# Attention and feed-forward in one kernel: score and state products of four pairs joined into one piece of TensorE work each

## The chip, the cores and the metric

The kernel runs on one core of one Trainium2 chip. The time is the device time of one execution in microseconds; the median of three executions is given, and a profiled execution is used to see where the time goes. Engines are named as in the profile: PE is TensorE (matmul), PEld its weight load, DVE VectorE, ACT ScalarE, POOL GpSimd, SP the engine that issues most DMAs.

## The reference

Linear attention with a decay per head, followed by a feed-forward block that is computed per token. The inputs are q, k and v of 4 batches, 8 heads, 768 tokens and 64 channels, in float32.

```python
for b in range(nb):                       # blocks of 64 tokens
    intra = einsum('bhic,bhjc->bhij', qb, kb) * Dmask      # scores, masked and decayed
    intra = einsum('bhij,bhjd->bhid', intra, vb)
    inter = einsum('bhid,bhde->bhie', qb * lam_pow, kv_state)
    out[:, :, sl] = intra + inter
    kv_state = lam_block * kv_state + einsum('bhsd,bhse->bhde', kb * rev_pow, vb)
x = out.transpose(0, 2, 1, 3).reshape(4, 768, 512)
xn = (x - mean(x)) / sqrt(var(x) + 1e-6) * g_ln
out = x + relu(xn @ w_ch1) @ w_ch2        # 512 -> 2048 -> 512
```

## The kernel before

The work is cut into 12 units of 256 tokens of one batch, called pairs here because each is a pair of 128-token chunks (`ab` 0 and 1); they are counted from 0, so the third to sixth are pairs 2 to 5. Pair u belongs to batch u mod 4, and the state of a batch is handed from pair u to pair u + 4. The steps of a pair are:

- loads of k, q and v by DMA from SP, in float32 (`load_in`, L76 and L80);
- scaling and conversion to bf16: `in_k_one` (L229, L213), `in_q_one` (L234) and `in_v` (L240), on POOL, ACT or DVE, into the tiles `kq` and `vb`;
- transposing k and q: by PE in pairs 0 to 2 (`transpose_pe`), by DMA from SP in the others (`transpose_dma`, L255, one DMA for k and one for q), into `kqT`;
- state products `kv` (L305): 32 matmuls in 64x64 tiles of the array, into two PSUM buffers `pk`. The argument names the buffers: "mm" is a rotating set of four that the feed-forward products use too, "po" are the two buffers of the attention's output;
- score products `scores` (L271), in two halves of 16 matmuls, also in 64x64 tiles, into two buffers of the tag "sc", or with `early=True` into two of the "mm" set;
- `mask` (L281) on DVE, from PSUM to `mA`; two per half;
- `new_state`: DVE adds the new products to the old state (`state_sum`, L315, or L311 where there is no old state), and POOL applies the decay (L311);
- `av` (L417) and `inter` (L430): the attention's output in `po`, again in 64x64 tiles;
- `norm`: ACT copies `po` to `x` with a row sum (L456), DVE forms `xc` (L458);
- `to_xT`: transposing `xc` for the feed-forward block; by PE (L491) into a "po" buffer in pairs 2, 3 and 4 with a copy by ACT (L492), by DMA (L484) from pair 5 on;
- `rstd_of`: the row's standard deviation on ACT (L501, L502), its reciprocal on DVE (L506).

Pairs 6 to 11 use other forms of the same steps (`kv64` L370, `scores64` L351, `av64` L404).

The feed-forward block of a pair is a list of units: `m1` (L528, 8 matmuls over the whole array, and a relu on ACT, L531) and, for pairs 0 to 3, `m2` (L665, 4 matmuls with 512 columns; after the fourth unit DVE adds the residual in `finish`, L689). From pair 4 on the second product is done with seven half products instead of eight (`m2w`, L563), for which sums over the second weight are formed once on DVE (`w_sums`, L787 to L791). All of these units stand in one plan, and `units(n)` takes the next n of them.

The order of the instructions on each engine is the order in which the program calls these functions; it is written out by hand at the end of the kernel. Each engine works through its instructions in that order. So where a call stands decides what lies between two attention steps on PE, and also what stands behind what on DVE, ACT, POOL and in SP's queue of DMAs.

The calls around pair 3 show the manner (lines 1083 to 1099, the casts of pair 5 left out):

```python
    w_sums(1, 0)
    units(3)
    s1(3)        # kv, scores of the first half, new_state, masks
    store(0)
    units(2)
    s2(3)        # scores of the second half, masks
    units(1)
    ...
    units(1)
    s3(3)        # av, first part of inter
    units(1)
    s4(3)        # second part of inter, norm
```

Of the kernel before, what the change touches and what calls it, by code (L numbers as in the profile page):

```python
# [8 lines left out]
BF16 = mybir.dt.bfloat16  # L9
# [8 lines left out]
def kernel(  # L18
# [11 lines left out]
    nc = tc.nc  # L30
# [7 lines left out]
    NP = H // 2  # L38
# [13 lines left out]
    wk = ctx.enter_context(tc.tile_pool(name="wk", bufs=2))  # L52
# [9 lines left out]
    def mm_tile(shape, dtype, name):  # L62
        return ps.tile(shape, dtype, tag="mm", bufs=4, name=name)
# [126 lines left out]
    st = {}  # L190
# [60 lines left out]
    def transpose_dma(u, a):  # L251
        s = st[u]
        if "kqT" not in s:
            s["kqT"] = wk.tile([128, 2, NP, 2, 128], BF16, tag="kqT", bufs=3, name="kqT")
        nc.sync.dma_start_transpose(s["kqT"][:, a].rearrange("p b j t -> p (b j) t"),  # L255
                                    s["kq"][:, a].rearrange("p b j e d -> p (b j e d)"))

    def scores(u, hf, early=False):

        s = st[u]  # L260
        kT, qT = s["kqT"][:, 0], s["kqT"][:, 1]
        if early:
            sc = [mm_tile([128, 2, 2, 128], F32, f"sce{e}") for e in range(2)]
        else:
            sc = [ps.tile([128, 2, 2, 128], F32, tag="sc", bufs=2, name=f"sc{e}") for e in range(2)]
        mA = wk.tile([128, 2, 2, 2, 128], BF16, tag=f"mA{hf}", name=f"mA{hf}")
        for i in range(2):
            for jk in range(2):
                for ab in range(2):
                    for e in range(2):  # L270
                        nc.tensor.matmul(sc[e][half[ab], i, jk, :], lhsT=kT[half[e], 2 * hf + i, jk, half[ab]],  # L271
                                         rhs=qT[half[e], 2 * hf + i, :, half[ab]],
                                         start=(i == 0 and jk == 0), stop=(i == 1 and jk == 1), skip_group_check=True)
        s[f"mA{hf}"] = mA
        s[f"sc{hf}"] = sc

    def mask(u, hf, heads=(0, 1)):
        s = st[u]
        kp = keep.rearrange("p a b t -> p a (b t)")
        for e in heads:  # L280
            nc.vector.tensor_tensor(s[f"mA{hf}"][:, e], s[f"sc{hf}"][e],  # L281
                                    kp[:, None, :, :].to_broadcast([128, 2, 2, 128]), op=ALU.mult)
# [11 lines left out]
    def kv(u, tag="mm"):  # L294

        s = st[u]
        cc, b = divmod(u, B)
        n_ab = 2 if (cc + 1) * W < S else 1
        bufs = dict(mm=4, sc=2, po=1)[tag]
        pk = [ps.tile([128, 2, NP, D], F32, tag=f"po{ab}" if tag == "po" else tag, bufs=bufs, name=f"pk{ab}")[:, 0] for ab in range(n_ab)]  # L300
        for p in range(NP):
            for j in range(2):
                for e in range(2):
                    for ab in range(n_ab):
                        nc.tensor.matmul(pk[ab][half[e], p, :], lhsT=s["kq"][half[ab], 0, p, j, e],  # L305
                                         rhs=s["vb"][half[ab], 2 * p + e, j],
                                         start=(p == 0 and j == 0), stop=(p == NP - 1 and j == 1), skip_group_check=True)
        s["pk"] = pk

    def decay(eng, dst, src):  # L310
        eng.tensor_tensor(dst, src, lam_s[:, :, None].to_broadcast([128, NP, D]), op=ALU.mult)  # L311
# [6 lines left out]
    def new_state(u, ab, eng):  # L318

        s = st[u]  # L320
        b = u % B
        if ab == 1 and len(s["pk"]) == 1:
            return
        old = state.get(b)
        if ab == 0:
            s["S"] = [(old, old)]
        Sn = wk.tile([128, NP, D], BF16, tag="S", bufs=12, name="Sn")
        if old is None and eng is nc.scalar:
            for p in range(NP):
                nc.scalar.activation(Sn[:, p], s["pk"][ab][:, p], ACT.Identity, scale=lam_s[:, p:p + 1])  # L330
        elif old is None:
            decay(nc.vector, Sn, s["pk"][ab])
        else:
            tmp = s.pop("tmp", None) or state_sum(u, ab)
            decay(eng, Sn, tmp)
        state[b] = Sn
        if ab == 0:
            s["S"].append((Sn, Sn))
# [136 lines left out]
    def to_xT(u, ab):  # L475
        s = st[u]
        t = 2 * u + ab
        g = group_of[t]
        i = t - groups[g][0]
        if i == 0:  # L480
            xT_of[g] = gp.tile([128, KA, GT * 128], BF16, tag="xT", bufs=3, name="xT")
        dst = xT_of[g][:, :, i * 128:(i + 1) * 128]
        if u >= 2 and u not in X_PE:
            nc.sync.dma_start_transpose(dst, s["xc"][:, ab])  # L484
        else:
            if u < 2:
                xt = mm_tile([128, KA, 128], BF16, "xt")
            else:
                xt = ps.tile([128, KA, 128], BF16, tag=f"po{ab}", name="xt")
            for kk in range(KA):  # L490
                nc.tensor.transpose(xt[:, kk, :], s["xc"][:, ab, kk * 128:(kk + 1) * 128], ident)  # L491
            nc.scalar.copy(dst, xt)  # L492

    def rstd_of(u):
        s = st[u]
        std = wk.tile([128, 2], F32, tag="std", name="std")
        if "sum" in s:
            ss = xp.tile([128, 2], F32, tag="ss", name="ss")
            for ab in range(2):
                sq = wk.tile([128, DM], BF16, tag="sq", bufs=1, name="sq")  # L500
                nc.scalar.activation(sq, s["x"][:, ab], ACT.Square, bias=s["nmean"][:, ab:ab + 1], accum_out=ss[:, ab:ab + 1])  # L501
            nc.scalar.activation(std, ss, ACT.Sqrt, bias=eps_t, scale=XS * XS / DM)  # L502
        else:
            nc.scalar.activation(std, s["mv"][:, :, 1], ACT.Sqrt, bias=eps_t, scale=XS * XS)
        rstd = xp.tile([128, 2], F32, tag="rstd", name="rstd")
        nc.vector.reciprocal(rstd, std)  # L506
        x_keep[u] = (s["x"], rstd)
# [187 lines left out]
    def store(u):  # L695
        for j in range(2):
            nc.sync.dma_start(rows_of(u)[j], o_of[u][half[j]])
# [83 lines left out]
    def w_sums(c, n):  # L781
        v = w2[c].rearrange("p (k e) d -> p k e d", e=2)
        w = DM // 2
        b11, b12, b21, b22 = v[:, :, 0, 0:w], v[:, :, 0, w:], v[:, :, 1, 0:w], v[:, :, 1, w:]
        t1, t2, t3, t4 = (wt[c][:, :, i] for i in range(4))
        if n == 0:
            nc.vector.tensor_tensor(t1, b12, b11, op=ALU.subtract)  # L787
            nc.vector.tensor_tensor(t3, b12, b22, op=ALU.add)
        else:
            nc.vector.tensor_tensor(t2, b11, t3, op=ALU.subtract)  # L790
            nc.vector.tensor_tensor(t4, t2, b21, op=ALU.add)  # L791
# [19 lines left out]
    def s0(u):  # L811
        kv(u, "po")
        new_state(u, 0, nc.gpsimd)
        new_state(u, 1, nc.gpsimd)
# [5 lines left out]
    def s1(u):  # L820
        kv(u)
        scores(u, 0)
        new_state(u, 0, nc.gpsimd)
        mask(u, 0, (0,))
        new_state(u, 1, nc.gpsimd)
        mask(u, 0, (1,))

    def wind_up(u):
# [22 lines left out]
        for ab in range(2):  # L851
            x, xh = s["x"][:, ab], s["x"][:, ab].rearrange("p (a e d) -> p a e d", e=2, d=D)
            nc.scalar.copy(x, s["po"][ab].rearrange("p h d -> p (h d)"))
            if has[ab]:
# [7 lines left out]
            nc.vector.scalar_tensor_tensor(s["xc"][:, ab], in0=x, scalar=s["mv"][:, ab, 0:1], in1=g_row,  # L862
                                           op0=ALU.subtract, op1=ALU.mult)

    def s2(u):
        scores(u, 1)
        mask(u, 1)
# [11 lines left out]
    def s4(u):  # L879
        inter(u, 1)  # L880
        if st[u]["S"][0][1] is not None:
            norm(u, 0)
        norm(u, 1)
# [142 lines left out]
    def units(n):  # L1026
        for _ in range(n):
            f, *a = next(steps)
            f(*a)
# [9 lines left out]
    s1b(2)  # L1039
    units(2)  # L1040
    s2(2)
    nc.scalar.activation(sqrt_first, eps_t, ACT.Sqrt)
    rstd_of(0)
    rstd_of(1)
    units(2)
    s0(2)
    open_window(3)
    in_k_one(3, nc.gpsimd, 0)
    in_k_one(3, nc.gpsimd, 1)
# [32 lines left out]
    units(2)  # L1082
    w_sums(1, 0)
    units(3)
    s1(3)
    store(0)
    units(2)
    s2(3)
    units(1)
    open_window(5)  # L1090
    in_k_one(5, nc.gpsimd, 0)
    in_k_one(5, nc.gpsimd, 1)
# [4 lines left out]
    s3(3)  # L1097
    units(1)
    s4(3)
    rstd_of(3)  # L1100
    open_in(6, False)
    load_in(6, "k", nc.sync)
    units(1)
    load_in(6, "q", nc.sync)
    units(1)
    w_sums(1, 1)
    load_in(6, "v", nc.sync)
    units(1)
    transpose_dma(5, 0)
    units(1)  # L1110
    to_xT(3, 0)
    transpose_dma(5, 1)
    open_in(7, False)
    load_in(7, "k", nc.sync)
    units(1)
    s1(4)
    to_xT(3, 1)
    open_window(6)
    in_k_one(6, nc.scalar, 0)
    units(1)  # L1120
    in_k_one(6, nc.gpsimd, 1)
    units(2)
    open_window(7)
    s2(4)
    units(2)
    s3(4)
    units(1)
# [11 lines left out]
    units(1)  # L1139
    open_in(8, False)  # L1140
    to_xT(4, 0)
    units(1)
    to_xT(4, 1)
    s1(5)
    units(1)
    transpose_dma(6, 1)
    units(1)
    in_q_one(7, nc.gpsimd, 0)
    units(1)
    in_q_one(7, nc.gpsimd, 1)  # L1150
    s2(5)
    transpose_dma(6, 0)
    units(2)
    rstd_of(4)
# [124 lines left out]
    in_k_one(11, nc.scalar, 0)  # L1279
    units(1)  # L1280
    in_k_one(11, nc.scalar, 1)
    transpose_dma(11, 0)
    transpose_dma(11, 1)
    units(1)
    m2s[8].sums(0, 4)
    units(1)
# [71 lines left out]
```

## Time and profile before

| | |
|---|---|
| time, median of 3 | 210.82 us (210.16 to 210.96) |
| the profiled execution | 209.44 us, its span 207.7 us |
| mean granted TensorE clock | 0.995 |
| PE busy | 197.0 us, 95% of the span |
| DVE, ACT, POOL busy | 134.3, 121.5, 86.0 us |
| bytes moved | 36.39 MB, 175 GB/s on average |

The span is the time from the first to the last instruction in the profiled execution. The chain of work that ended last is followed back from the last instruction, at each step to what released it; a row of it gives a start, a duration and what it was. Rows of a timeline give start, duration, engine, line, operation, output and inputs, and in brackets how long the engine had stood idle and what ended that. Starts and durations are in us from the start of the span. The chain counts each instruction only from the moment at which it is the one that matters, so its pieces lie end to end; the timeline gives each instruction's whole duration, and those overlap on PE.

### The profile page before, as it was taken

How to read it: one execution, taken by the hardware profiler on the slowest of the kernel's cores; microseconds unless marked ns; L12 is line 12 of the kernel's file. 1: busy time of each engine (PE TensorE's matmuls, PEld its weight loads, DVE VectorE, ACT ScalarE, POOL GpSimd, SP SyncE). 2: the span in 40 equal slices, each digit the busy share in tenths (PEclk: the TensorE clock that was granted, in tenths of full speed). 3: DMA queues.
4: the chain of work that ended last, by engine and by line, in shares of the span. 5: the costliest groups of instructions: out<-in, count | busy, mean ns of one | idle time of the engine just before them, and what ended most of it. 6: DMA issues, size and time to landing. Idle time of an engine off the chain costs nothing.

```text
span 207.7 us, 7234 instructions
## 1 busy us (share of the span) xinstructions
PE 197.0 (95%) x3099; PEld 156.3 (75%) x3099; DVE 134.3 (65%) x274; ACT 121.5 (58%) x279; POOL 86.0 (41%) x119
## 2 busy tenths in 40 slices
PE   2989999999999999999999999999999999999991
PEld 0468788545774587488888888888888888888880
DVE  2588350625864949767898775786877947855262
ACT  3776479535357457257565775585586565752620
POOL 5558049237784540635264441772182202001020
PEclk9999999999999999999999999999999999999997
DMA  4999999999898999996899999898957020268403
GB/s 106 299 257 218 193 269 186 187 289 260 202 261 248 228 137 229 188 290 109 180 199 145 190 196 173 211 190 145 227 98 171 4 51 3 28 157 273 105 13 90
DMA packets 91042, 36.39 MB, mean 175 GB/s; under 512 B 65153, under 2 KB 88193, under 8 KB 91010
## 3 DMA queue, kind: packets, MB, share of 16 engines
q1 hardware_dynamic: 86400, 31.53, 74.1%
q0 software_dynamic: 4224, 4.19, 12.7%
q8 instruction: 24, 0.39, 0.8%
q10 hardware_dynamic: 386, 0.20, 0.4%
q14 instruction: 8, 0.07, 0.1%
HBM read 27.27 MB, written 6.29 MB: 162 GB/s over the span
## 4 chain that ended last, share of the span: by engine, by line
PE 84%; DMA 5%; DVE 4%; ACT 3%; issue 1%; POOL 0%; POOLq 0%; DVEq 0%
PE pm L528 38%; PE pm L665 14%; PE pwd L563 6%; PE pwa L563 6%; PE pwc L563 6%; DMA w<-in_moe_w_ch_dram 3%; PE pwb L563 3%; DMA lam_b<-in_lam_dram 2%; PE po L417 2%; PE po L430 1%; PE tp L248 1%; PE sc L271 1%; DVE x L576 1%; PE po L404 1%; PE sc L351 1%
## 5 line engine op out<-in xcount | busy, mean ns | idle before, releaser
L528 PE MATMUL pm<-xT,w 128*128 128x256 bf16 x736 | 85.1, 273 | 0.6 <-DMA w<-in_moe_w_ch_dram 0.4
L528 PEld LDWEIGHTS <-w 128*128 128x128 bf16 x736 | 70.3, 98 | 10.5 <-DMA w<-in_moe_w_ch_dram 0.6
L531 ACT ACTIVATE hT<-pm 128x512 f16<-128x512 f32 x92 | 54.0, 599 | 32.6 <-PE pm L528 32.5
L665 PE MATMUL pm<-w,hT 128*128 128x512 f16 x128 | 30.2, 380 | 0.0
L588 POOL TENSOR_TENSOR x<-ev_u,x 128x256 f32<-128x256 f32 x8 | 5.8, 725 | 51.8 <-ACT ev_u L587 40.5
L563 PEld LDWEIGHTS <-hs 128*128 128x128 f16 x256 | 24.9, 98 | 2.9
L546 DVE TENSOR_TENSOR hs<-hT 128x1024 f16<-128x1024 f16 x16 | 14.1, 881 | 16.6 <-ACT hT L531 16.6
L311 POOL TENSOR_TENSOR Sn<-Stmp,lam_s 128x256 bf16<-128x256 f32 x16 | 9.8, 616 | 31.4 <-DVE Stmp L389 18.4
L665 PEld LDWEIGHTS <-hT 128*128 128x128 f16 x128 | 11.7, 98 | 12.1
L563 PEld LDWEIGHTS <-hT 128*128 128x128 f16 x192 | 18.8, 98 | 2.2
L281 DVE TENSOR_TENSOR mA<-sc,keep 128x512 bf16<-128x512 f32 x20 | 13.1, 684 | 10.4 <-PE sc L271 10.3
L458 DVE SCALAR_TENSOR_TENSOR xc<-po,nmean,g_row 128x512 bf16<-128x512 f32 x18 | 13.0, 746 | 5.0 <-ACT nmean L457 4.9
L456 ACT ACTIVATE x<-po 128x512 f32<-128x512 f32 x18 | 10.6, 590 | 8.0 <-PE po L430 4.5
L240 POOL TENSOR_TENSOR vb<-vin,lam_v 128x1024 bf16<-128x1024 f32 (+1 forms) x7 | 11.6, 1659 | 5.0 <-DMA vin<-in_v_dram 4.8
L240 POOL TENSOR_TENSOR vb<-vin,lam_p 128x1024 bf16<-128x1024 f32 x6 | 11.7, 1954 | 3.4 <-DMA vin<-in_v_dram 3.4
L501 ACT ACTIVATE sq<-x,nmean 128x512 bf16<-128x512 f32 x18 | 12.9, 718 | 0.3
L576 DVE SCALAR_TENSOR_TENSOR x<-pwd,rstd,x 128x256 f32<-128x256 f32 x16 | 7.7, 482 | 3.6 <-POOL x L596 3.6
L234 POOL TENSOR_TENSOR kq<-qin,lam_p 128x512 bf16<-128x512 f32 x9 | 9.3, 1042 | 1.1 <-DMA qin<-in_q_dram 1.1
L234 POOL TENSOR_TENSOR kq<-qin,lam_q 128x512 bf16<-128x512 f32 x8 | 8.6, 1089 | 2.8 <-DMA qin<-in_q_dram 2.8
L576 DVE SCALAR_TENSOR_TENSOR x<-pwa,rstd,x 128x512 f32<-128x512 f32 (+1 forms) x16 | 9.1, 613 | 0.8
L563 PE MATMUL pwa<-w,hT 128*128 128x256 f16 x64 | 9.6, 272 | 0.0
L563 PE MATMUL pwb<-w,hT 128*128 128x256 f16 x64 | 9.2, 272 | 0.0
(131 smaller groups left out, 297.5 us busy)
## 6 DMA issues: line engine op xcount, KB each, us to landing
out_dram<-x SPq DMA_DIRECT2D x22, 256.0 KB, 3.9
w<-in_moe_w_ch_dram POOLq DMA_DIRECT2D x8, 512.0 KB, 7.8
kin<-in_k_dram SPq DMA_DIRECT2D x14, 256.0 KB, 5.3
qin<-in_q_dram SPq DMA_DIRECT2D x14, 256.0 KB, 4.8
vin<-in_v_dram SPq DMA_DIRECT2D x14, 256.0 KB, 5.1
kin<-in_k_dram SPq DMA_DIRECT2D x5, 512.0 KB, 6.2
qin<-in_q_dram SPq DMA_DIRECT2D x5, 512.0 KB, 7.0
vin<-in_v_dram SPq DMA_DIRECT2D x5, 512.0 KB, 7.8
```

The lines of the kernel that those rows point to most:

```text
L234: eng.tensor_tensor(part(1, st[u]["kq"], ALL)[:, :, :, j], src[:, :, :, j], lq[:, :, :, None].to_broadcast([128, NP, 2, D]), op=ALU.mult)
L240: eng.tensor_tensor(st[u]["vb"][:, hs], qkv_in[u]["v"][:, hs], lv.to_broadcast([128, n, 2, D]), op=ALU.mult)
L281: nc.vector.tensor_tensor(s[f"mA{hf}"][:, e], s[f"sc{hf}"][e], kp[:, None, :, :].to_broadcast([128, 2, 2, 128]), op=ALU.mult)
L456: nc.scalar.activation(x, po, ACT.Copy, accum_out=sm)
L458: nc.vector.scalar_tensor_tensor(xc, in0=po, scalar=nm, in1=g_row, op0=ALU.add, op1=ALU.mult)
L501: nc.scalar.activation(sq, s["x"][:, ab], ACT.Square, bias=s["nmean"][:, ab:ab + 1], accum_out=ss[:, ab:ab + 1])
L528: nc.tensor.matmul(pm[:, b, :], lhsT=w1[n // W2K][:, kk, (n % W2K) * 128:(n % W2K + 1) * 128], rhs=xT_of[g][:, kk, 0:N], start=(b == 0 and ...
L531: nc.scalar.activation(hT[:, u * NB:(u + 1) * NB, 0:N], pm, ACT.Relu)
L546: nc.vector.tensor_tensor(s13, b[:, :, 1:2, :].to_broadcast([128, n, 2, 128]), b[:, :, 0:4:3, :], op=ALU.subtract)
L563: nc.tensor.matmul(pr[bank], lhsT=lhs(r), rhs=rhs, start=(first and r == 0), stop=(r == KB // 2 - 1), skip_group_check=True)
L576: nc.vector.scalar_tensor_tensor(out, in0=in0, scalar=r[ab], in1=in1, op0=ALU.mult, op1=ALU.add)
L665: nc.tensor.matmul(acc[i], lhsT=hT[:, kk, i * 128:(i + 1) * 128], rhs=w2[kk // W2K][:, kk % W2K, :], start=(kk == 0), stop=(kk == KB - 1))
```

## The change

Pairs 3, 4 and 5 get a new step `s12` in place of `s1` and `s2`. It issues the state products, both halves of the scores, and then the masks and the state updates. The state products go to the "po" buffers instead of "mm", and the first half's scores to "mm" instead of "sc". The units that stood between the halves follow behind them or move ahead of them. In pair 2 the state step `s0` moves ahead of two units and of the reciprocals of pairs 0 and 1, to directly behind `s2`. For this, the second transpose of pairs 3 and 4 (`to_xT(3, 1)`, `to_xT(4, 1)`) moves ahead, directly behind the first, and `w_sums(1, 1)` moves ahead of pair 3's `rstd_of`. In pair 11 one DMA transposes both k and q, where there were two. The number of matmuls and of the other engines' operations stays the same.

In the line numbers of the changed kernel everything behind `transpose_dma` stands 6 lines lower and everything behind `wind_up` 15 lines lower (at the end of the kernel by a few lines less).

```diff
+    def transpose_both(u):
+        s = st[u]
+        s["kqT"] = wk.tile([128, 2, NP, 2, 128], BF16, tag="kqT", bufs=3, name="kqT")
+        nc.sync.dma_start_transpose(s["kqT"].rearrange("p a b j t -> p (a b j) t"),
+                                    s["kq"].rearrange("p a b j e d -> p (a b j e d)"))
...
+    def s12(u):
+        kv(u, "po")
+        scores(u, 0, early=True)
+        scores(u, 1)
+        mask(u, 0)
+        new_state(u, 0, nc.gpsimd)
+        mask(u, 1)
+        new_state(u, 1, nc.gpsimd)
...
     s2(2)
+    s0(2)
     nc.scalar.activation(sqrt_first, eps_t, ACT.Sqrt)
     rstd_of(0)
     rstd_of(1)
     units(2)
-    s0(2)
     open_window(3)
...
     w_sums(1, 0)
     units(3)
-    s1(3)
+    s12(3)
     store(0)
-    units(2)
-    s2(3)
-    units(1)
+    units(3)
     open_window(5)
...
     s4(3)
+    w_sums(1, 1)
     rstd_of(3)
...
     units(1)
-    w_sums(1, 1)
     load_in(6, "v", nc.sync)
     units(1)
     transpose_dma(5, 0)
     units(1)
     to_xT(3, 0)
+    to_xT(3, 1)
     transpose_dma(5, 1)
     open_in(7, False)
     load_in(7, "k", nc.sync)
-    units(1)
-    s1(4)
-    to_xT(3, 1)
+    units(2)
+    s12(4)
     open_window(6)
     in_k_one(6, nc.scalar, 0)
-    units(1)
     in_k_one(6, nc.gpsimd, 1)
     units(2)
     open_window(7)
-    s2(4)
     units(2)
     s3(4)
...
     to_xT(4, 0)
-    units(1)
     to_xT(4, 1)
-    s1(5)
-    units(1)
+    units(2)
+    s12(5)
     transpose_dma(6, 1)
...
     in_q_one(7, nc.gpsimd, 1)
-    s2(5)
     transpose_dma(6, 0)
...
     in_k_one(11, nc.scalar, 1)
-    transpose_dma(11, 0)
-    transpose_dma(11, 1)
+    transpose_both(11)
     units(1)
```

## The prediction

> **What bounds the kernel now.** I read the page first, then the chain that ended last, then the timelines of DVE, ACT, POOL and SP between 35 and 90 us, then the waits. Pairs are counted as in the code, from 0, so the change touches pairs 2 to 5 and pair 11.
>
> ```profile
> PE 197.0 (95%) x3099; PEld 156.3 (75%) x3099; DVE 134.3 (65%) x274; ACT 121.5 (58%) x279; POOL 86.0 (41%) x119
> ```
>
> PE is busy for 197.0 of 207.7 us, and the chain runs on PE from 28 us to 197 us almost without a break. DVE has a third of the span free. What shortens PE's own row of work between 35 and 90 us therefore shortens the kernel, as long as nothing else turns up late. The chain there:
>
> ```profile
> 53.84 3.49 PE pm L528 x32
> 57.33 0.38 PE pk L305 x32
> 57.71 0.23 PE sc L271 x16
> 57.94 1.85 PE pm L528 x16
> 59.79 0.39 PE sc L271 x16
> 60.18 1.85 PE pm L528 x16
> 62.03 0.64 PE po L417 x64
> ...
> 69.03 0.23 PE sc L271 x16
> 69.26 0.33 PE xt L491 x4
> 69.59 1.73 PE pm L665 x8
> 71.32 0.87 PE pm L528 x8
> 72.19 0.35 PE sc L271 x16
> 72.54 1.85 PE pm L528 x16
> 74.39 0.68 PE po L417 x64
> ```
>
> Columns: start, us, what. The same 16 score products (L271) take 0.23 us when they follow the state products (L305), which also use 64x64 tiles, and 0.35 or 0.39 when they follow 128x128 products. The other side shows too: 16 products of L528 take 1.85 us behind a small piece, but 32 take 3.49 where none stands ahead, that is 1.745 for 16; the transposes of L491 take 0.33 behind scores, and 0.22 elsewhere in the chain. So each change between small tiles and the whole array costs about 0.12 us going in and 0.10 us coming out.
>
> ```profile
> 57.77 0.42 DVE L311 TENSOR_TENSOR Sn<-pk,lam_s 128x256 bf16<-128x256 f32 x1 [1.13 <-PE pk L305]
> 58.11 0.68 DVE L281 TENSOR_TENSOR mA<-sc,keep 128x512 bf16<-128x512 f32 x1
> 58.70 0.41 DVE L315 TENSOR_TENSOR Stmp<-pk,Sn 128x256 f32<-128x256 f32 x1
> 59.03 0.68 DVE L281 TENSOR_TENSOR mA<-sc,keep 128x512 bf16<-128x512 f32 x1
> 60.22 1.29 DVE L281 TENSOR_TENSOR mA<-sc,keep 128x512 bf16<-128x512 f32 x2 [0.50 <-PE sc L271]
> ...
> 66.97 1.68 DVE L790 TENSOR_TENSOR wt<-w,wt 128x512 f16<-128x512 f16 x1
> ```
>
> This is DVE's work on pair 3: a mask takes 0.60 us from start to start, a state sum 0.33, and the first mask starts 0.04 us after the scores end.
>
> **The change, part by part.** (a) Pair 2: the state products move from between two groups of L665 to directly behind its second scores. Before, from 38.29: scores 0.35, 8 products 1.83, state 0.38, 8 products 1.83 = 4.39. After: 0.35, state at its inner price 0.38 - 0.11 = 0.27, 16 products behind a small piece 3.56 (the chain has this at 64.01) = 4.18. Gain 0.21.
> (b) Pair 3: before, 57.33 to 62.03 = 4.70. After: state 0.38, scores 0.23 and 0.23, 32 products of L528 behind a small piece 3.60 (the chain at 76.42) = 4.44. Gain 0.26, of which 0.04 is a wait: the second scores stood until DVE's mask ended at 59.71.
> (c) Pair 4: before, 67.57 to 74.39 = 6.82. After: eight transposes 0.44, 8 products 1.73, state 0.38, scores 0.46, 4 products 0.97 (as at 62.80), 24 of L528 2.62 (1.5 times 1.745) = 6.60. Gain 0.22; joining the transposes brings nothing of its own, the 0.11 behind the scores is one of the borders counted. The 0.68 of L417 instead of 0.64 may give 0.04 more.
> (d) Pair 5: before, 80.02 to 88.54 = 8.52. After: 4 products 0.86, transposes 0.44, 8 products 1.73, state 0.38, scores 0.46, 20 products 4.43 (2.70 for 12 behind a small piece, and 8 at 1.73) = 8.30. Gain 0.22.
> Sum: 0.21 + 0.26 + 0.22 + 0.22 + 0.04 = 0.95 us.
>
> A rule speaks against this. The Trainium skill, TensorEngine Tiling (Array Packing), Instruction Overhead, puts about 60 cycles on each matmul and none on a border; no instruction is removed, so by it the sum would be 0. The rows at 57.71 and 59.79 are the same 16 instructions at 0.23 and 0.39 us, so I take the rows.
>
> **What covers the rest.** The joined piece gives DVE all its work at once: two masks, a sum, two masks, a sum. By the order of the instructions the first two matmuls of L417 now wait for the two sums, the second of which is the last thing DVE does; before, L417 waited for masks halfway in. Counted from the first state product of pair 3: the first scores end at 0.61, DVE starts at 0.65, and 4 x 0.60 + 0.33 later starts the last sum, which ends 0.41 after that, at 3.79. L417 comes up on PE at 0.84 + 3.60 = 4.44. Margin 0.65. Pair 4: 4.43 against 3.79, the same margin. Pair 5: 0.84 + 4.43 = 5.27, margin 1.5. Pair 2's masks keep their place and its two sums have 3.56 us of products to hide behind. Here a second rule weighs against the change: the same page, PSUM Bottleneck, says that emptying PSUM can become the limit once tiling speeds TensorE up, and to split it between ScalarE and VectorE; here VectorE does all of it. Had it no cover, each piece would wait some 3 us, 9 us over pairs 3 to 5; the rows give it 3.6 to 4.4 us of cover, so I take 0.
> The scores of the first half now hold the two rotating buffers that the state products held; the L528 tiles that reuse them start 2.7 us after the first state product and need only the first two masks, done at 1.9. The state products use the buffers of the outputs instead. In pairs 4 and 5 these wait for ACT's two copies of the transposes (0.58 each), covered by the 8 products of 1.73: margin about 0.6, and one for one on the path if ACT comes later than that. The transposes that move ahead read DVE's results of 65.76 and 79.2, in time for 67.6 and 80.9. In pair 2 they need POOL's v product, done at 36.29, against 38.6.
> Queues: ACT's and POOL's orders do not change, but POOL waits behind the sums. State update L311 comes about 2 us later in pairs 3, 4 and 5, and the casts and products behind it with it. Pair 5's k and q work then ends near 65 us and its transpose goes at 72.39; pair 7's q products end near 89, its transpose goes at 95. The second product of pair 2's residual waits on DVE behind the masks of pair 4 (73 instead of 71.8); no buffer that it frees is asked for before L417. The earlier sums over w2 (L790, L791) fall into a time when DVE waited for ACT's std (until 66.89), and free DVE before the scores of pair 4.
> (e) Pair 11's transposes:
>
> ```profile
> 153.74 2.63 SPq L255 DMA_TRANSPOSE kqT<-kq  x2
> ```
>
> Each landed 3.1 us after its issue, the second near 158.2. One DMA with both: at best as before, at worst the two landings in a row, 6.2 us, 159.9. The scores that read it come at 162.5, or 161.6 after the gain. Neither end reaches the path, for no work waits there now: I take 0, and a gain is excluded for the same reason; behind it in SP's queue stand only stores, and the transposes that wait for DVE until 165.55.
> After 90 us nothing changes but the time: the transposed operands there land 2 to 4 us ahead of their use, so an earlier PE of 0.95 us still finds them.
> The profiled execution took 209.44 us (span 207.7), below the lowest of the three timed ones, 210.16. Its time would become 208.49; I carry the difference to the median: 210.82 - 0.95 = 209.87, forecast 209.9.
>
> **Rivals.** *Borders dearer than the chain shows.* The waits name PEld L271 held by issue for 1.9 us in 7 times, 0.27 each. If that is what a piece costs going in, with 0.10 coming out, four pieces give 4 x 0.37 = 1.5 us: 209.3. For it: the row. Against: at 59.79 the whole piece takes only 0.16 more than its neighbour.
> *DVE becomes the bound.* Slower than before. The place is the first L417 of pairs 3 and 4, with their margins of 0.65. If DVE's 3.1 us of masks and sums stretch by half, 1.6 us, each of the two pairs waits 0.95, the gain is used up and 0.95 lost: 211.8 with pair 5 touched as well. It decides from a stretch of about a third on (1.1 of 3.1 us), where waits equal gains. For it: L790 took 1.68 us while POOL worked beside it, and 0.43 elsewhere. Against: masks read PSUM, and all 22 took 678 to 692 ns.
> *The joined transpose is late.* Above 7.9 us to land, PE waits at pair 11 one for one; to be slower by 1 us it must take 9.9, three times a landing. Near 211.5 if so.
> *Nothing happens*, the borders being an artefact of modelled ends: 210.8.
>
> **How the numbers follow.** About 0.5%, 1.05 us, is what a measurement of this kernel can tell from no change; that is 209.77, just below the forecast. Forecast 0.68, with its own range 209.3 to 210.5 (each border read to 0.02 us, medians of three moving 0.4); it splits evenly, 0.34 faster and 0.34 the same. Dearer borders 0.16, nearly all faster. Nothing happens 0.05, the same. DVE the bound 0.08, joined transpose late 0.03, together all of the slower. Sums: 0.50 faster, 0.39 the same, 0.11 slower. Range 208.9 to 211.3: below it takes in 1.5 us of gain with a low median, above it the case of no gain and half of the DVE case.
>
> **What would show it.** In the chain after: behind L305 two groups of L271, together some 0.46, no L271 of 0.35 between products in pairs 3 to 5, and from the start of pair 2's second scores to pair 5's first L417 some 49.3 us where it was 50.25 (88.54 - 38.29). In the DVE rows: sums ending 0.6 us ahead of L417. Wrong would be: L417 of pair 3 or 4 waiting for DVE L315 (now another line number), state products waiting for ACT's copies, the pair 11 scores waiting for SP, or pieces that shrink without the rows after them moving.

## The result, and the profile after

The changed kernel took 209.25 us (median of 8, 207.99 to 210.09) against 210.31 us (median of 8, 209.34 to 211.06) for the kernel before in the same sitting: ratio 0.9936, 95% interval 0.9913 to 0.9959. Two more comparisons, in later sittings, gave 0.9970 (0.9949 to 0.9991) and 0.9956 (0.9933 to 0.9978); they are `e0_after` and `e10_after_again` below. The mean of the three is 0.9954, which is 0.97 us of 210.3. The kernel is faster by about half a per cent; the first figure alone makes it look larger than the three together do. Ratios here and below leave out executions that took over 1.5% longer than the fastest of the same kernel. The profiled execution took 208.88 us, with a span of 207.2 us.

In the chain that ended last (start, us, what), the rows of pairs 2, 3, 4 and 5 are now these (`...` stands for rows left out). Line numbers are 6 higher than before: L277 for L271, L311 for L305, L423 for L417, L534 for L528, L671 for L665. `sce` is the buffer of the first half's scores, `sc` that of the second's.

```profile
38.62 0.35 PE sc L277 x16
38.97 0.28 PE pk L311 x32
39.25 3.56 PE pm L671 x16
42.81 0.64 PE po L423 x64
...
57.47 0.37 PE pk L311 x32
57.84 0.23 PE sce L277 x16
58.07 0.22 PE sc L277 x16
58.29 3.60 PE pm L534 x32
61.89 0.64 PE po L423 x64
...
67.43 0.45 PE xt L497 x8
67.88 1.73 PE pm L671 x8
69.60 0.37 PE pk L311 x32
69.98 0.23 PE sce L277 x16
70.20 0.22 PE sc L277 x16
70.43 0.97 PE pm L671 x4
71.40 2.62 PE pm L534 x24
74.02 0.64 PE po L423 x64
...
79.62 0.86 PE pm L671 x4
...
82.65 0.37 PE pk L311 x32
83.03 0.23 PE sce L277 x16
83.25 0.24 PE sc L277 x16
83.49 4.42 PE pm L671 x20
87.91 0.64 PE po L423 x64
```

In pairs 3 to 5 the second scores take 0.22 to 0.24 us where they took 0.35 and 0.39, since they follow work in the same tiles, and one row of full-array products instead of two carries the extra 0.10. In pair 2 the state products take 0.28 us behind the scores, where they took 0.38 between full-array products. DVE's rows of pair 3 in the timeline after, and the last sums of pairs 4 and 5:

```profile
58.11 1.29 DVE L287 TENSOR_TENSOR mA<-sce,keep 128x512 bf16<-128x512 f32 x2 [1.55 <-PE sce L277]
59.32 0.42 DVE L317 TENSOR_TENSOR Sn<-pk,lam_s 128x256 bf16<-128x256 f32 x1
59.65 1.28 DVE L287 TENSOR_TENSOR mA<-sc,keep 128x512 bf16<-128x512 f32 x2
60.84 0.41 DVE L321 TENSOR_TENSOR Stmp<-pk,Sn 128x256 f32<-128x256 f32 x1
...
72.98 0.42 DVE L321 TENSOR_TENSOR Stmp<-pk,Sn 128x256 f32<-128x256 f32 x1
...
86.14 0.42 DVE L321 TENSOR_TENSOR Stmp<-pk,Sn 128x256 f32<-128x256 f32 x1
```

The last sum of pair 3 ends at 60.84 + 0.41 = 61.25, and L423 begins at 61.89. DVE has all the masks and sums to do at once, and is still done 0.64 us early. In pair 4 it is 74.02 - 73.40 = 0.62 us early, in pair 5 87.91 - 86.56 = 1.35. L796, which took 1.68 us as L790 at 66.97, took 0.42 at 65.53: POOL's v product (L240), which ran beside it before, from 66.46 on, starts at 66.77 here, after it.

**A measure that leaves the start out.** The starts of these rows differ from one execution to the next: pair 2's second scores start between 38.07 and 40.15 us, in one profile at 41.83. I therefore compare one stretch in all profiles, from the start of pair 2's second scores to the start of pair 5's L417 or L423. In the chain before, its ends are

```profile
38.29 0.35 PE sc L271 x16
...
88.54 0.64 PE po L417 x64
```

It was 88.54 - 38.29 = 50.25 us before and 87.91 - 38.62 = 49.29 us after: 0.96 us less.

### The profile page after: what moved, and what is told of

The parts are those of the page before. It is cut to its first block, busy times and chain, and to the rows that moved or that the text cites. A ratio compares the mean times of both kernels' runs of the same rounds, so it can differ in the third digit from the quotient of the medians.

```text
span 207.2 us, 7235 instructions
## 1 busy us (share of the span) xinstructions
PE 196.1 (95%) x3099; PEld 156.4 (75%) x3099; DVE 132.9 (64%) x274; ACT 121.4 (59%) x279; POOL 85.3 (41%) x119
## 3 DMA queue, kind: packets, MB, share of 16 engines
q0 software_dynamic: 4224, 4.19, 12.7%
## 4 chain that ended last, share of the span: by engine, by line
PE 84%; DMA 5%; DVE 4%; ACT 3%; issue 1%; POOL 0%; POOLq 0%; DVEq 0%
PE pm L534 38%; PE pm L671 14%; PE pwd L569 6%; PE pwa L569 6%; PE pwc L569 6%; DMA w<-in_moe_w_ch_dram 3%; PE pwb L569 3%; DMA lam_b<-in_lam_dram 2%; PE po L423 2%; PE po L436 1%; PE tp L248 1%; DVE x L582 1%; PE po L410 1%; PE sc L357 1%; PE pm1t L645 1%
## 5 line engine op out<-in xcount | busy, mean ns | idle before, releaser
L534 PE MATMUL pm<-xT,w 128*128 128x256 bf16 x736 | 84.8, 273 | 0.8 <-issue 0.5
L534 PEld LDWEIGHTS <-w 128*128 128x128 bf16 x736 | 70.4, 98 | 10.5 <-issue 0.8
L671 PE MATMUL pm<-w,hT 128*128 128x512 f16 x128 | 29.8, 380 | 0.0
L569 PEld LDWEIGHTS <-hs 128*128 128x128 f16 x256 | 24.8, 98 | 3.0
L552 DVE TENSOR_TENSOR hs<-hT 128x1024 f16<-128x1024 f16 x16 | 14.3, 891 | 17.0 <-ACT hT L537 17.0
L671 PEld LDWEIGHTS <-hT 128*128 128x128 f16 x128 | 11.8, 98 | 12.5
L569 PEld LDWEIGHTS <-hT 128*128 128x128 f16 x192 | 18.7, 98 | 2.2
L287 DVE TENSOR_TENSOR mA<-sc,keep 128x512 bf16<-128x512 f32 x14 | 9.0, 684 | 9.6 <-PE sc L277 9.6
L240 POOL TENSOR_TENSOR vb<-vin,lam_v 128x1024 bf16<-128x1024 f32 (+1 forms) x7 | 11.6, 1656 | 3.9 <-DMA vin<-in_v_dram 3.8
L240 POOL TENSOR_TENSOR vb<-vin,lam_p 128x1024 bf16<-128x1024 f32 x6 | 11.4, 1896 | 1.9 <-DMA vin<-in_v_dram 1.9
L569 PE MATMUL pwa<-w,hT 128*128 128x256 f16 x64 | 9.6, 273 | 0.0
L569 PE MATMUL pwb<-w,hT 128*128 128x256 f16 x64 | 9.2, 273 | 0.0
```

What stands on the lines that cost most here:

```text
L240: eng.tensor_tensor(st[u]["vb"][:, hs], qkv_in[u]["v"][:, hs], lv.to_broadcast([128, n, 2, D]), op=ALU.mult)
L534: nc.tensor.matmul(pm[:, b, :], lhsT=w1[n // W2K][:, kk, (n % W2K) * 128:(n % W2K + 1) * 128], rhs=xT_of[g][:, kk, 0:N], start=(b == 0 and ...
L552: nc.vector.tensor_tensor(s13, b[:, :, 1:2, :].to_broadcast([128, n, 2, 128]), b[:, :, 0:4:3, :], op=ALU.subtract)
L569: nc.tensor.matmul(pr[bank], lhsT=lhs(r), rhs=rhs, start=(first and r == 0), stop=(r == KB // 2 - 1), skip_group_check=True)
L671: nc.tensor.matmul(acc[i], lhsT=hT[:, kk, i * 128:(i + 1) * 128], rhs=w2[kk // W2K][:, kk % W2K, :], start=(kk == 0), stop=(kk == KB - 1))
```

## The experiments

Each was timed against the kernel before in five rounds, and each was profiled once. The stretch named above is given as "the stretch".

**The changed kernel again** (`e0_after`, no edit).

> The changed kernel itself, as the measure for the other runs on this chip. Theory (borders between 64x64 tiles and the whole array, four pieces saved at 0.22 us and two short waits, 0.95 us in all): ratio 0.9955. Rival, dearer borders (0.37 us a piece, 1.5 us): 0.993. Rival, the time lies elsewhere and the pieces bring nothing: 1.000 here, or a gain that e1 alone shows.

Ratio 0.9970 (0.9949 to 0.9991), stretch 49.27 us. In the three profiles of this kernel the stretch repeats to 0.02 us. In the five kernels below whose edits lie behind it, it was 49.27 twice, 49.38, 49.50 and 49.74, so a single profile can be 0.5 us too long; all are below the 50.21 and 50.25 of the order before. The ratio lies within what 0.95 us would make, and its interval leaves out the 0.993 of dearer borders.

**The joined transpose alone** (`e1_joined_dma`), on the kernel before.

```diff
-    transpose_dma(11, 0)
-    transpose_dma(11, 1)
+    transpose_both(11)
```

> The kernel before with one part of the change alone: pair 11's k and q transposed by one DMA. Theory: nothing waits for it, ratio 1.000 within 0.1%; the joined DMA lands between 3.1 and 6.2 us after its issue at about 153.7, before 160, and the scores that read it still start at 162.5. Rival, that the part of the gain beyond 0.95 us comes from this DMA: ratio 0.998, with something behind it in SP's queue some 0.4 us earlier and a PE row that moves with it.

Ratio 0.9996 (0.9971 to 1.0020), stretch 50.21 us, as before. The profiled execution of this run took 212.48 us, 2 us above its median, and its rows begin some 3.5 us later than in the other; the stretch does not show it. This part brings nothing that can be measured. In the changed kernel's profile the DMA took SP 1.66 us to issue from 153.5 on, where the two took 2.63, and landed 4.3 us after its issue, at 157.8. The scores that read it come at 162.2, more than 4 us after that.

**The pieces cut in three** (`e2_three_pieces`), in the changed kernel; the units that follow `s12` are fewer by as many.

```diff
     def s12(u):
         kv(u, "po")
+        new_state(u, 0, nc.gpsimd)
+        new_state(u, 1, nc.gpsimd)
+        units(1)
         scores(u, 0, early=True)
-        scores(u, 1)
         mask(u, 0)
-        new_state(u, 0, nc.gpsimd)
+        units(1)
+        scores(u, 1)
         mask(u, 1)
-        new_state(u, 1, nc.gpsimd)
```

> The changed kernel with the pieces of pairs 3, 4 and 5 cut in three each: state products, one feed-forward unit, scores of the first half, one unit, scores of the second half; the state sums right behind the state products. Six pieces more than the changed kernel, the same products. Theory: 6 x 0.225 = 1.35 us slower than e0_after, which is 1.002 of the kernel before; in the chain each scores row 0.35 and each row behind it 0.10 longer. Rival, dearer borders: 6 x 0.37 = 2.2 us slower than e0_after. Rival, no cost of borders: the time of e0_after.

Ratio 1.0039 (1.0014 to 1.0064), that is 0.0069 or 1.45 us above `e0_after` on the same chip. The stretch is 90.06 - 39.28 = 50.78 us, 1.51 more than in `e0_after`, 0.25 a piece. The chain of this kernel for pair 3:

```profile
58.12 0.38 PE pk L311 x32
58.50 0.98 PE pm L534 x8
59.48 0.35 PE sce L277 x16
59.83 0.98 PE pm L534 x8
60.81 0.35 PE sc L277 x16
61.15 1.85 PE pm L534 x16
63.01 0.64 PE po L423 x64
```

The same instructions as in the changed kernel, and each row is dearer by just what the prediction took: 0.35 for 0.22 or 0.23, and 0.98 where 8 of these products took 0.87 with nothing small ahead (71.32 in the chain before). The edit also changes DVE's order. No wait of PE for DVE shows in these rows, but in pair 4 the second masks end at 75.83 and L423 begins at 75.59: L423 takes 0.69 and the following L436 0.21 us, 0.13 more than in the changed kernel. Without this wait a piece cost (1.51 - 0.13) / 6 = 0.23 us, where 0.225 was expected. Both rivals fall: the cost is not nothing, and it is not the 0.37 of dearer borders.

**Pair 6 in one piece** (`e3_pair6_joined`).

```diff
-    X1(6)
+    X(6)
...
-    X2(6)
```

> The changed kernel with pair 6 treated as pairs 7 to 10 are: outputs of pair 5, state products and scores of pair 6 and the second inter products in one piece, where two L534 units stood between. One piece fewer. Theory: 0.22 us faster than e0_after, ratio to the kernel before 0.9945; L357 at 0.25 to 0.29 in the chain where it was 0.37. Rival, that DVE, which gets two sums and a mask ahead of the norm of pair 5 at once, holds up what follows: the time of e0_after or more, with a PE wait between 90 and 95 us.

Ratio 0.9960 (0.9936 to 0.9983), not to be told from the changed kernel. The joined scores took 0.32 us rather than the 0.25 to 0.29 I expected. From the start of pair 5's L423 to the first half product (L569) this profile has 98.19 - 88.62 = 9.57 us, no less than the 97.39 - 87.91 = 9.48 of the changed kernel: what was saved was given back at a stop of PE of 0.68 us at 94, which in the profile of the changed kernel was 0.53 long. That stop is the next question; it is in the chain of the changed kernel,

```profile
91.34 2.07 PE pm L534 x18
93.41 0.53 issue
93.95 3.45 PE pm L534 x30
```

in that of the kernel before, one matmul further on in PE's order,

```profile
94.22 0.12 issue
94.34 3.34 PE pm L528 x29
```

and in the busy times of a stretch of 1 us of the changed kernel (length, then busy us and instructions of PE, PEld, DVE, ACT and POOL, then PE clock, DMA share, GB/s):

```profile
93.00:94.00 1.00, 0.47 (x5) 0.18 (x4) 0.96 (x3) 0.98 (x3) 1.00 (x1) 1.00 1.04 399
```

PE is busy for 0.47 of the 1 us from 93 on, while it waits for no other engine, its clock is at full speed, and the DMA engines move 399 GB/s. Among the bytes are those of the four stores of pairs 1 and 2, issued from 88.26 to 91.8. The DMA records show an instruction transfer of 16 KB (queue q8) from 91.19 to 92.52, and PE goes on at 93.95, 1.4 us after its end.

**The stores later** (`e6_stores_later`), in the changed kernel.

```diff
-    store(1)
-    store(2)
     to_xT(5, 0)
...
     to_xT(5, 1)
+    store(1)
+    store(2)
```

> The changed kernel with the stores of pairs 1 and 2 (1 MB) issued behind the second transpose of pair 5's residual rows instead of ahead of the first, at about 100 us instead of 88. In two profiles of the changed kernel PE stood 0.50 and 0.53 us at about 93, in the one of the kernel before 0.12, at the same place in PE's order, 1.3 us after an instruction transfer of the DMA engines ended, and while these moved 380 to 400 GB/s. Theory A (the instruction transfer is held up by the stores): the stop at 93 shrinks to 0.15 or nothing, 0.4 us faster than the changed kernel. Theory B (the stop belongs to the place in the instruction stream, where many small matmuls use up instructions quickly, whatever the DMAs do): it stays at 0.5, and the time of the changed kernel stays.

In this profile the stop is gone; PE runs through where it stood:

```profile
92.95 5.39 PE pm L534 x48
```

But the kernel is slower: ratio 1.0061 (1.0033 to 1.0088). From the start of pair 5's L423 to the first half product it took 98.35 - 89.53 = 8.82 us against 9.48 in the changed kernel. What it loses comes later: the q and v loads of pair 8 stand behind the stores in SP's queue. POOL's timeline and PE's waits in this kernel:

```profile
109.50 2.49 POOL L234 TENSOR_TENSOR kq<-qin,lam_p 128x512 bf16<-128x512 f32 x2 [1.15 <-DMA qin<-in_q_dram]
113.67 1.90 POOL L240 TENSOR_TENSOR vb<-vin,lam_p 128x1024 bf16<-128x1024 f32 x1 [1.67 <-DMA vin<-in_v_dram]
```

```profile
PE pwc L569 <- DVE hs L552: 1.3, 2, 0.8
...
PE pm L534 <- DVE Smid L392: 0.5, 1, 0.5
```

In the changed kernel POOL's products of these two ran at 107.35 and 109.35 without a wait for the loads. Counted from pair 5's L423, v's product starts at 24.1 us here and at 21.4 there, 2.7 us late. It then runs beside DVE's sums of the hidden layer (L552 takes 2.24 us at 113.87, and 0.69 in the changed kernel at 112.91) and holds up the state steps behind it on POOL. PE waits for DVE at 116.2 (0.8 us) and at 123.9 (0.5), and a third time at 146.6 (0.6), behind the next group of stores and a q load: 1.8 us in all. The gain in time that I drew from theory A is not there.

Nor is theory A shown for the stop. If the stores held up the instruction transfer, it would be shorter without them. It took 1.27 us here (92.21 to 93.48) and 1.32 to 1.33 in the three profiles of the changed kernel. Here the DMA engines moved little beside it (64 GB/s from 92 to 93, nothing from 93 to 94), while in `e2_three_pieces`, with the stores at their old place, it took 1.06 us (93.12 to 94.17) beside 389 GB/s, and PE did not stop:

```profile
93.00:94.00 1.00, 1.00 (x11) 0.89 (x10) 1.00 (x3) 0.97 (x5) 0.61 (x2) 1.00 0.00 0
```

```profile
93.00:94.00 1.00, 1.00 (x54) 0.87 (x53) 0.76 (x2) 1.00 (x3) 0.51 (x2) 1.00 1.06 389
```

The first row is of this kernel, the second of `e2_three_pieces`. What differs is when the transfer comes: it begins 2.7 us after pair 5's L423 here, and 3.2 to 3.3 us after it in the changed kernel. Why it does is open. Theory B, that the stop stays whatever the DMAs do, does not fit this profile either.

**Both together** (`e7_joined_and_stores`: the edits of `e3_pair6_joined` and `e6_stores_later`).

> Pair 6 in one piece as in e3_pair6_joined, and the stores of pairs 1 and 2 later as in e6_stores_later. By theory A of e6 the stop of 0.68 us at 94 in e3 goes, and the piece saved counts: 0.6 us faster than the changed kernel, ratio 0.9925 against the kernel before. By theory B the stop stays, and the ratio is that of the changed kernel, 0.995 to 0.997.

Ratio 1.0066 (1.0038 to 1.0093): slower too, with the stores in the same place of SP's queue. The chain of this kernel runs through the four stores (98.98 to 101.98), the load of v behind them (landed at 112.2) and POOL's v product (112.33), and PE waits 2.0 us for DVE in all. Neither theory's ratio came, since both left out that queue. And with all four stores moved, the matmul at which PE stands still came 0.15 us late here: 0.256 us after the one before it, where the pace is 0.109.

**More work for DVE** (`e4_dve_one` and `e5_dve_four`), in the changed kernel; the second edit adds `mask(u, 1)` twice instead.

```diff
         mask(u, 1)
+        mask(u, 1, (0,))
         new_state(u, 1, nc.gpsimd)
```

> The changed kernel with one mask of the second half done a second time (same result) ahead of the last state sum of pairs 3, 4 and 5: 0.60 us more on DVE in each. Theory (DVE has 0.64 and 0.62 us to spare in pairs 3 and 4, 1.35 in pair 5): no cost, the ratio of the changed kernel, 0.995 to 0.997; the last sums end within 0.1 us of the first L423 of pairs 3 and 4. Rival, DVE is already the bound there: 1.2 to 1.8 us slower than the changed kernel, ratio 1.002.

Ratio 0.9947 (0.9928 to 0.9967): no cost that the time shows. The last sums end at 62.68 and 74.89, within 0.03 us of the start of L423, as expected. L423 shows where the spare time ends, for it takes 0.76 and 0.72 us in pairs 3 and 4 instead of 0.64, a wait of about 0.1 us; the stretch, 49.48 us, has these 0.2 us more.

> The same with both masks of the second half done twice more: 2.4 us more on DVE in each of the pairs 3, 4 and 5. Theory: PE waits 1.75, 1.75 and 1.05 us for the last sums, 4.55 us together, ratio about 1.018 against the kernel before. Rival, the sums do not hold up PE as the order of waits says (the masks alone count, halfway into L423): 1.0 us or more less in all, ratio below 1.012.

Ratio 1.0186 (1.0168 to 1.0204), and a stretch of 92.19 - 38.07 = 54.12 us, 4.85 more than in `e0_after`, where 4.55 were expected. The chain has moved from PE to DVE in pair 3:

```profile
57.35 0.28 PE sce L277 x16
57.63 1.28 DVE mA L287 x2
58.91 0.33 DVE Sn L317
59.24 3.58 DVE mA L287 x6
62.82 0.34 DVE Stmp L321
63.17 0.04 issue
63.21 0.70 PE po L423 x63
```

L423 waits for the last state sum and not for the masks; only its first matmul runs ahead, and the stretch is counted here to the row of the other 63. The rival of the prediction in which DVE sets the end exists, and starts where the margin of 0.6 us is used up; the changed kernel is on the near side of it.

**One store later** (`e8_one_store_later`), and the changed kernel beside it (`e10_after_again`, no edit).

```diff
-    store(1)
     store(2)
     to_xT(5, 0)
...
     load_in(9, "k", nc.sync)
+    store(1)
```

> The changed kernel once more, as the measure beside the two runs that follow. Theory: 0.95 us less than the kernel before, less what the stop at 93 us gives back (0.4): ratio 0.9955 to 0.998. Rival: dearer borders, 0.993. In the profile a stop of some 0.5 us on L534 near 93.

> The changed kernel with one of the two stores in question (pair 1) moved behind the load of pair 9's k, near 106 us, where SP's queue stood 1.3 us; pair 2's store stays near 88. In e6 the stop at 93 was gone, but the q and v loads of pair 8 stood behind the stores, and POOL and PE waited for them. Theory: the stop near 93 shrinks below 0.2 us and no new wait of PE comes, since only 0.5 us is added to what stands behind in SP's queue: 0.3 us faster than the changed kernel, ratio 0.995. Rival: half the bytes hold up the instruction transfer as well, the stop stays near 0.5. Second rival: 0.5 us more in SP's queue is enough to make POOL late, PE waits between 113 and 124.

The changed kernel: 0.9956 (0.9933 to 0.9978), stretch 49.27 us, a stop of 0.29 us. With one store later: 0.9981 (0.9956 to 1.0005), stretch 49.27, a stop of 0.27 us. The stop did not shrink below the one beside it, so the theory's 0.3 us did not come; PE waits for no other engine between 113 and 124, so the second rival did not come either. The stop itself was 0.53, 0.50 and 0.29 us in three profiles of one kernel, so one profile cannot tell 0.1 us here, and moving one store brings nothing to be seen in the time.

**The same with pair 6 joined** (`e9_joined_one_store`: the edits of `e3_pair6_joined` and `e8_one_store_later`).

> The same store moved, with pair 6 in one piece as in e3_pair6_joined. Theory: 0.5 us faster than the changed kernel, ratio 0.993 to 0.994. Rival: the stop stays at 0.6 to 0.7 as in e3, ratio 0.996.

No stop at this place in the profile,

```profile
90.78 7.18 PE pm L534 x64
```

and from pair 5's L423 to the first half product 8.72 us, the shortest of all. `e6_stores_later`, which had no stop either but pair 6 in two pieces, took 8.82: joining pair 6 is worth about 0.10 us at this place, less than half of the 0.22 expected. The stretch ahead of it took 49.74 us, with a wait of PE for DVE (L695, 0.2 us) ahead of pair 3. The ratio is 0.9955 (0.9927 to 0.9983), that of the changed kernel on the same chip, and not the 0.993 to 0.994 expected. No version beat the changed kernel in time.

## Why the prediction was right, and where it was not

- *The cost of a border* (0.12 us in, 0.10 out, four pieces). Right. The stage sums, forecast and measured in the chain after, are 4.18 and 4.19 for pair 2 (38.62 to 42.81), 4.44 and 4.42 for pair 3, 6.60 and 6.59 for pair 4, 8.30 and 8.29 for pair 5. L423 of pair 4 took 0.64 instead of 0.68, the 0.04 that was put down as possible. Sum 0.95 forecast, 0.96 in the stretch. Cutting the pieces again (`e2_three_pieces`) cost 0.25 a piece, 0.23 without a wait for DVE. The price holds for these pieces: at pair 6 a joined piece saved 0.10. What takes the time inside a border, the array's change of tiling or the first weights behind it, was not tested. The rule of the Trainium skill on a price per matmul (TensorEngine Tiling (Array Packing), Instruction Overhead) would by itself have made the sum 0, and the runs decide against it as an account of this gain: the number of matmuls never changed, and the rows did. No run here measured the price of a single matmul against it.
- *DVE in time.* Right: 0.64, 0.62 and 1.35 us to spare, where 0.65, 0.65 and 1.5 were worked out. The rule on emptying PSUM (same page, PSUM Bottleneck) comes into force once the cover is gone, as `e5_dve_four`, with more reads of PSUM by DVE, shows with 4.85 us; with the cover as it is, it costs nothing.
- *The joined transpose at nothing.* Right; its landing of 4.3 us lies between the two ends that were given.
- *Nothing changes after 90 us but the time.* This step failed in part. The profile of the changed kernel had gained 0.63 us by pair 5's L423 (88.54 to 87.91), although its row had begun 0.33 later; of this 0.29 was left at the first half product (97.68 to 97.39). The difference is the stop at 93, 0.53 us long for 0.12. I had looked at whether operands land in time, and not at PE's own instructions. The matmul at which PE stands never began earlier than 1.3 us after an instruction transfer ended, in any profile. PE came to it about 0.7 us earlier than before, at 93.25 instead of 93.94, and the transfer ended only 0.45 us earlier, at 92.52 instead of 92.97. How much of it the average execution gives back stays open, because the stop varies from one profile to the next; the mean ratio of the three comparisons leaves no more than a few tenths of a microsecond for it.
- *The number.* Forecast 209.9 us, measured 209.25. Of the 0.65 us between them 0.51 is the starting point: the forecast set out from a median of three, 210.82, and the median of eight is 210.31. That the mean gain of the three comparisons, 0.97, lies so near to 0.95 is in part luck: from their intervals I estimate that it is known to about 0.3 us, and part of the gain is lost at the stop.
- *The rivals.* Dearer borders (0.37 a piece) are ruled out by `e2_three_pieces`, DVE did not set the end, the joined transpose landed long before 7.9 us, and borders that are only modelled would not have moved the time. The forecast's own bound of 0.5% lay, as said, at the edge: the first measurement came out beyond it, the other two within.

## What to carry to other kernels

Where PE is the bound, look in the chain for the same instructions at two prices: the difference belongs to what stands ahead of them, and joining pieces in the same tiling can save it without removing an instruction; read at each place what it saves, for here it was 0.23 us in one stage and 0.10 in another. Before joining, add up what the engine that empties PSUM now gets at once, and compare that with the full-array work up to the first wait for its last result, not its average load. And a gain on the bound engine makes it arrive earlier at everything further on, its own instruction transfers too. Before moving a DMA out of the way, check what stands behind its new place in the queue, since that may be nearer to its need than it looks.

## What the runs showed of the hardware that was not expected

- PE can stand for 0.1 to 1.4 us with no wait for another engine, at a fixed place in its order, and goes on 1.3 to 1.5 us after an instruction transfer of 16 KB has ended. One such place is the 1502nd matmul (the 1503rd in the kernel before), at about 93 us: seven of the thirteen profiles show a stop there, of 0.12 to 0.68 us, and in `e7_joined_and_stores` that matmul came 0.15 us late; in these eight PE went on 1.30 to 1.46 us after the transfer's end. In the other five PE came to it 1.37 us after that end or later. The second is the 352nd matmul, at about 24 us: eight profiles show a stop of 0.19 to 1.43 us, ended 1.27 to 1.49 us after a transfer. Both come behind runs of small matmuls, 160 within 3.4 us at the first; whether using up instructions that fast is what exposes the transfer was not tested.
- The stores, beside which the DMA engines moved 399 GB/s, are not shown to be the cause: the transfer took no less time when they were moved away (1.27 us in `e6_stores_later`, 1.31 in `e7_joined_and_stores`), and three profiles with the stores at their old place show no stop (`e1_joined_dma`, `e2_three_pieces`, `e5_dve_four`).
- One DMA that transposes k and q took 1.66 us to issue and 4.3 us to land, against 2.63 us for the issue of two and 3.1 us for the landing of each in the kernel before.
